# First step of the polynomial exponential on GpSimd, 32-bit shift and root times quadratic on VectorE, eight tiles a batch

## The chip, the cores and the metric

The kernel runs on one core of a Trainium2 chip. TensorE multiplies matrices into PSUM; ScalarE, VectorE and GpSimd work on tiles of 128 partitions; the DMA queues of SyncE, ScalarE and GpSimd move data. The metric is the device time of one execution in microseconds; a profile of one execution comes beside it. In the profile PE is TensorE, ACT is ScalarE, DVE is VectorE, POOL is GpSimd, SP is SyncE.

## The reference

Softcapped attention over 8 batches of 12 heads, 448 tokens, head size 64, then a soft mixture of experts with 32 slots:

```python
scores = cap * np.tanh(scale * np.matmul(q, k.T) / cap)          # cap = 30
attn = np.exp(scores - scores.max(-1)); attn /= attn.sum(-1) + 1e-09
x = np.matmul(attn, v)                    # as 3584 tokens x 768
logits = x @ phi                          # 32 slots
d = softmax of logits over the tokens; c = softmax of logits over the slots
slot_out[e] = np.maximum((d.T @ x)[e] @ w1[e], 0) @ w2[e]         # 8 experts, 4 slots each
out = c @ slot_out
```

## The kernel before

**Tiling.** A pair is two heads side by side, a quad is two pairs; there are 48 pairs. The scores of a pair come transposed, keys on partitions, in seven tiles of 128 x 448 (the line `NT = 7`). The 336 tiles are handled in 56 chunks of six, so a batch of the input (six pairs) is seven chunks, and what stands in chunk j recurs in chunk j + 7. A chunk's tiles live in one of five `ex` buffers.

**Stages of a chunk.** TensorE makes the scores of three tiles at a time (`qk_chunk`, L316) into one of two PSUM buffers `sc`. ScalarE applies tanh to the three (`tanh_chunk`, L325) and writes `ex`. One chunk later it exponentiates `ex` in place (`exp_chunk`, L329), but leaves the first `taken(j)` tiles of the chunk to VectorE. Two chunks later TensorE multiplies `ex` by V: `pv_first` does the first four tiles of a pair, `pv_rest` the others (both L385), into a single PSUM buffer of the pool `psV`. V lies in two buffers `vbd`, filled by a GpSimd cast (L286). `norm` ends a pair on VectorE: a reciprocal of the sums (L392) and a product into `xq` (L395). Then come transposes of `xq` (copied by VectorE into `xT`, L446), the logits, their exponential on ScalarE (L471), its copy on GpSimd (L477), and sums over the tokens. q and k are loaded by GpSimd's queue (L186), turned on TensorE and copied by VectorE (L278); all these turnings share one PSUM buffer, `psT`. The weights are loaded by GpSimd's queue, one or two blocks a chunk (L116, L120). After the last chunk come the two layers of the experts and the output.

**Order.** The order of the work is written by hand. The main loop runs over the chunks, and between its steps it calls slots, named `0`, `m`, `e`, `a`, `b`, `r`, `c`, `d` in this order; each slot has a part before it (`<a`) and one after it (`>a`). `at(j, slot, f, ...)` hangs a piece of work on a slot of chunk j. Each engine executes its instructions in this order and waits on semaphores; nothing is moved at run time. `FILL` hangs matrix products that compute nothing on some slots.

**The polynomial on VectorE.** From chunk 3 to chunk 53, one tile in each chunk is exponentiated with five VectorE instructions (`poly_exp`): `e` is the argument scaled to base 2 and written as a 32-bit integer (L362); the upper 16 bits shifted left by 7 are the bits of a bf16 power of two `b` (L364); the lower 16 bits are the fraction `f`, and three instructions (L365 to L367) make `((f + p2) f`, then `(. + p1) f`, then `(. + p0) b`, which is written to `ex`. There is one set of work buffers. `PARTS` says for each chunk of a batch in which slots the five stand.

**Weights.** `KEPT` blocks of w2 stay in SBUF; the others are written to DRAM as bf16 and loaded again after attention (`w2t`).

Of the kernel before, what the change touches and what calls it, by code (L numbers as in the profile page):

```python
# [9 lines left out]
F32 = mybir.dt.float32  # L10
BF16 = mybir.dt.bfloat16
I32 = mybir.dt.int32
U16 = mybir.dt.uint16
ALU = mybir.AluOpType
# [3 lines left out]
P = 128  # L18
HP = 64
NT = 7  # L20
DH = 64
S = 448
CH = 6
# [7 lines left out]

FRAC = 2.0 ** 16
POW2 = (0.07802398, 0.22606796, 0.69583329, 0.99992523)


@with_exitstack
def kernel(
# [12 lines left out]
    B, H, _, _ = q.shape  # L50
# [7 lines left out]
    cap = float(cap)  # L58
    qk_scale = 1.0 / (DH ** 0.5)

    NQB = H // 4
# [1 line left out]
    NPAIR = 2 * NQ  # L63
    NTILE = NPAIR * NT
    NCH = NTILE // CH
    KEPT = 11

    ctx.enter_context(tc.manual_schedule())
    pe, dve, act, pool, sp = nc.tensor, nc.vector, nc.scalar, nc.gpsimd, nc.sync
# [28 lines left out]
           for e in range(E - 2)]  # L98
    w2b = wts.tile([P, KEPT, 4, HD], BF16, name="w2b")

# [23 lines left out]
    w2_parts = [(n0, half) for n0 in range(0, len(blocks), 4) for half in range(2)]  # L124
    w2_kept, w2_spilled = w2_parts[:KEPT], w2_parts[KEPT:]

# [5 lines left out]

    att = ExitStack()
    ld = att.enter_context(tc.tile_pool(name="ld", bufs=1))
    NP = 1
    homes = {}
    for nm in ("qk0", "ex1", "wk", "ldv", "ex2", "ex3", "vb0", "qk1", "ex4", "ex0", "vb1"):
        homes[nm] = att.enter_context(tc.tile_pool(name=nm, bufs=1))
# [1 line left out]
    vb = [homes["vb0"], homes["vb1"]]  # L140
    qk = [homes["qk0"], homes["qk1"]]
    ldv, wk = homes["ldv"], homes["wk"]
    work = wk.tile([P, 5 * NP * S // 2], I32, name="work")
    xe, xp = work[:, 0:NP * S], work[:, NP * S:2 * NP * S].bitcast(F32)
    xb = work[:, 2 * NP * S:].bitcast(BF16)
    xs = att.enter_context(tc.tile_pool(name="xs", bufs=4))
    attp = ExitStack()
    psS = attp.enter_context(tc.tile_pool(name="psS", bufs=2, space=PSUM))
# [156 lines left out]
    scores, exs, pvs, xq, xTs, lps = {}, {}, {}, {}, {}, {}  # L305
# [25 lines left out]
    def exp_chunk(j):  # L331
        exp_part(j, taken(j), CH)

    PARTS = {0: (1, ((0, "<b", (0,)), (0, "<d", (1, 2)), (1, "a", (3,)), (1, "<b", (4,)))),
             1: (1, ((0, "<b", (0,)), (0, ">b", (1,)), (0, "c", (2,)), (1, "a", (3,)), (1, "<b", (4,)))),
             2: (1, ((0, "a", (0,)), (0, "<b", (1,)), (0, ">d", (2, 3)), (1, "a", (4,)))),
             3: (1, ((0, "a", (0,)), (0, "c", (1,)), (0, ">d", (2,)), (1, "<b", (3, 4)))),
             4: (1, ((0, ">b", (0,)), (0, "c", (1,)), (0, ">d", (2, 3)), (1, "a", (4,)))),  # L340
             5: (1, ((0, ">b", (0,)), (0, "c", (1,)), (1, "<b", (2,)), (1, ">b", (3,)), (1, "r", (4,)))),
             6: (1, ((0, ">b", (0,)), (0, "c", (1,)), (0, ">d", (2,)), (1, "a", (3,)), (1, ">b", (4,))))}
    shared = {j: (PARTS[j % 7],) for j in range(6, NCH - 6) if j % 7 in PARTS}
    shared.update({3: ((1, ((0, "a", (0,)), (0, "c", (1,)), (0, ">d", (2,)), (1, "<b", (3, 4)))),), 4: ((1, ((0, ">b", (0,)), (0, "c", (1,)), (0, ">d", (2, 3)), (1, "a", (4,)))),), 5: ((1, ((0, ">b", (0,)), (1, "a", (1, 2)), (1, "<b", (3,)), (1, ">b", (4,)))),), 50: ((1, ((0, "<b", (0,)), (0, "c", (1, 2)), (1, "a", (3, 4)))),), 51: ((1, ((0, "a", (0,)), (0, "<b", (1,)), (0, ">d", (2, 3)), (1, "a", (4,)))),), 52: ((1, ((0, ">b", (0,)), (0, "c", (1,)), (1, "a", (2,)), (1, "<b", (3, 4)))),), 53: ((1, ((0, ">b", (0,)), (0, "c", (1,)), (0, ">d", (2, 3)), (1, "a", (4,)))),)})
    if cap >= 50:
        shared = {}

    def taken(j):
        return sum(n for n, _ in shared.get(j, ()))

    lead = POW2[0] / FRAC ** 3
    p2, p1, p0 = (c / POW2[0] * FRAC ** (n + 1) for n, c in enumerate(POW2[1:]))
    halves16 = xe.bitcast(U16).rearrange("p (s two) -> p s two", two=2)
    frac, whole = halves16[:, :, 0], halves16[:, :, 1]

    def poly_exp(j, u, tiles, ops):
        n1 = tiles * S
        t = exs[j][:, u:u + tiles, :].rearrange("p u s -> p (u s)")
        e, p, b = xe[:, 0:n1], xp[:, 0:n1], xb[:, 0:n1]
        f, w = frac[:, 0:n1], whole[:, 0:n1]  # L360
        steps = (
            lambda: dve.tensor_scalar(e, t, cap * math.log2(math.e) * FRAC,  # L362
                                      (127 + math.log2(lead)) * FRAC, ALU.mult, ALU.add),
            lambda: dve.tensor_scalar(b.bitcast(U16), w, 7, None, ALU.logical_shift_left),  # L364
            lambda: dve.scalar_tensor_tensor(p, f, p2, f, ALU.add, ALU.mult),  # L365
            lambda: dve.scalar_tensor_tensor(p, p, p1, f, ALU.add, ALU.mult),  # L366
            lambda: dve.scalar_tensor_tensor(t, p, p0, b, ALU.add, ALU.mult))  # L367
        for n in ops:
            steps[n]()

# [171 lines left out]
    def at(j, slot, f, *a):  # L542
        if j < 0:
            j, slot = 0, "b"
        aux.setdefault((j, slot), []).append((f, a))
# [3 lines left out]
        busy(n, psV.tile([P, parts * P], F32, name="junk", tag="pv"))  # L549

    FILL = ((3, "a", fill, 2), (4, "a", fill, 14), (5, "a", fill, 10), (6, "a", spare, 10), (6, "c", spare, 12), (7, "a", fill, 16), (8, "a", fill, 20), (9, "a", fill, 6))
    PER = 2 * NQB * NT // CH
    assert PER == 7 and NQB == 3

    def quad_in(Q, cast_k, cast_q, k_in, q_in, v_in):
        if 0 < Q < NQ:
# [10 lines left out]
    for b in range(B):  # L567
        j, p = b * PER, 6 * b

        def when(nm):  # L570
            return j + WHEN[nm][0], WHEN[nm][1]
# [17 lines left out]
        if b < B - 1:  # L589
# [5 lines left out]
                at(*when("en"), e_norm, b)  # L595
            if b % 2:
                at(*when("es"), e_sums, b // 2)
    for j, groups in shared.items():
        u = 0
        for tiles, parts in groups:  # L600
            for dj, slot, ops in parts:
                at(j + dj, slot, poly_exp, j, u, tiles, ops)
            u += tiles
    for n, job in enumerate(wjobs):
        at(1 + n * (NCH - 5) // len(wjobs), "b", *job)
    for j, slot, n in ((0, "a", 10), (0, "c", 10), (1, "b", 10), (1, "c", 8)):
# [71 lines left out]
    assert place[last, 0] == NTILE - NT and pair_at[NCH - 3] == last - 2  # L678
    CL = CS
    exp_part(NCH - 1, taken(NCH - 1), CL)  # L680
    exp_part(NCH - 1, CL, CH - 1)
    exp_part(NCH - 1, CH - 1, CH)
# [102 lines left out]
    for n in range(12):  # L785
        a = n % 4 * NS
# [13 lines left out]
    for n0, half in sorted(w2_spilled, key=lambda x: (x[1], x[0])):  # L800
        t = tl.tile([P, 4, HD], BF16, name=f"w2t{n0}_{half}")
# [123 lines left out]
    for n in range(B // 2 * NT):  # L925
        bb, c = divmod(n, NT)
# [15 lines left out]
        if n == NH or c == 0 or full:  # L942
            ob, n1 = wts.tile([P, 2, 2, HD], F32, name="ob", tag="w1", bufs=E), n
# [44 lines left out]
```

## Time and profile before

| | |
|---|---|
| median of three runs | 302.41 us (301.85 to 303.36) |
| profiled execution: span from first to last instruction | 299.1 us |
| time of the profiled execution beside its span | not given separately; the median is 3.3 us above the span |
| TensorE, ScalarE, VectorE, GpSimd busy | 266.7, 265.7, 237.5, 139.0 us |
| exponentials on ScalarE (L329) | 58 instructions, 51 of them of five tiles |
| mean granted TensorE clock | 0.987 |

Times are microseconds from the start of the span. A busy time is the union of an engine's records; an engine's records can overlap, since the next one may start before the last has ended. A group row has the line, the engine, the operation, what it writes and reads, the shapes and the count, then busy time and mean ns of one, then the engine's idle time before them. A row of waits has the waiting engine and line, who ended the wait, the total, the count and the longest. A row of a timeline has start, duration, engine, line, operation and count. A stage row has the stretch, its length, and the busy time of PE, PEld, DVE, ACT and POOL, then the granted clock, the DMA share and GB/s.

### The profile page before, as it was taken

What the parts mean: (1) busy time and instruction counts of PE and PEld (TensorE: products, weight loads), DVE (VectorE), ACT (ScalarE), POOL (GpSimd) and SP (SyncE); (2) the same over time, 40 slices, a digit from 0 to 9 for tenths busy, and PEclk for the clock granted to TensorE, in tenths of its full rate; (3) what the DMA queues carried; (4) which work ended last, traced back from release to release, by engine and by line L of the source; (5) the groups of instructions that cost most, each with busy time, mean ns of one, the idle gap of its engine ahead of it and who ended that gap; (6) DMA issues with size and microseconds to landing.
All of it is one profiled execution on the core that took longest, in us unless ns stands there. A gap on an engine that the chain in (4) does not pass through costs nothing.

```text
span 299.1 us, 11031 instructions
## 1 busy us (share of the span) xinstructions
PE 266.7 (89%) x4821; PEld 179.3 (60%) x4821; DVE 237.5 (79%) x497; ACT 265.7 (89%) x211; POOL 139.0 (46%) x200
## 2 busy tenths in 40 slices
PE   8898989998999999989999999899999999999820
PEld 6655556755675667566756675667666767542410
DVE  3728989898999999999899989998998963336840
ACT  4999999999999999999999999999999997227730
POOL 4583554764566466745575547464653220300000
PEclk9999999999999999999999999999999999999995
DMA  7999999999999999999899999999999579929997
GB/s 230 260 192 205 200 192 205 186 198 221 229 194 181 206 231 215 197 211 227 164 179 216 228 214 183 216 228 219 192 185 223 113 246 343 400 110 354 406 422 291
DMA packets 58559, 68.12 MB, mean 228 GB/s; under 512 B 4240, under 2 KB 54672, under 8 KB 58512
## 3 DMA queue, kind: packets, MB, share of 16 engines
q0 software_dynamic: 42448, 35.31, 76.6%
q1 hardware_dynamic: 15776, 31.89, 30.3%
q8 instruction: 37, 0.61, 0.8%
q10 hardware_dynamic: 288, 0.23, 0.2%
q14 instruction: 10, 0.08, 0.1%
HBM read 91.72 MB, written 19.27 MB: 371 GB/s over the span
## 4 chain that ended last, share of the span: by engine, by line
ACT 41%; PE 32%; DVE 13%; issue 7%; POOL 2%; DMA 2%; DVEq 0%; SPq 0%; ACTq 0%
ACT ex L325 25%; ACT ex L329 13%; PE pv L385 9%; PE sc L316 5%; DVE xq L395 3%; PE so_ps L856 2%; PE hp L823 2%; PE kps L276 2%; POOL vbd L286 2%; DVE work L364 1%; PE qps L276 1%; PE xps L433 1%; PE pv L415 1%; DVE work L362 1%; ACT ob L948 1%
## 5 line engine op out<-in xcount | busy, mean ns | idle before, releaser
L325 ACT ACTIVATE ex<-sc 128x1344 bf16<-128x1344 f32 (+1 forms) x113 | 166.0, 1738 | 1.2 <-PE sc L316 1.2
L329 ACT ACTIVATE ex<-ex 128x2240 bf16<-128x2240 bf16 (+4 forms) x58 | 145.1, 2528 | 0.1
L385 PE MATMUL pv<-vbd,ex 128*128 128x130 bf16 (+1 forms) x1610 | 94.7, 211 | 8.6 <-POOL vbd L286 7.5
L385 PEld LDWEIGHTS <-ex 128*128 128x128 bf16 (+1 forms) x1680 | 76.0, 101 | 31.9 <-issue 9.2
L316 PE MATMUL sc<-qT,kT 64*64 64x448 bf16 x672 | 70.1, 359 | 2.5 <-ACT ex L325 1.9
L286 POOL CAST vbd<-vraw 64x896 bf16<-64x896 f32 x46 | 44.9, 977 | 51.1 <-PE pv L385 37.0
L366 DVE SCALAR_TENSOR_TENSOR work<-work 128x448 f32<-128x448 f32 x51 | 31.8, 623 | 1.2
L367 DVE SCALAR_TENSOR_TENSOR ex<-work 128x448 bf16<-128x448 f32 x51 | 31.8, 624 | 0.6
L365 DVE SCALAR_TENSOR_TENSOR work<-work 128x448 f32<-128x448 uint16 x51 | 31.7, 621 | 0.0
L395 DVE TENSOR_TENSOR xq<-pv,rec 128x448 bf16<-128x448 f32 x46 | 28.7, 625 | 1.6
L316 PEld LDWEIGHTS <-kT 64*64 64x64 bf16 x672 | 24.2, 105 | 7.7 <-issue 5.5
L477 POOL COPY e<-E 128x512 bf16<-128x512 bf16 x9 | 7.0, 778 | 43.0 <-PE eps L496 20.2
L364 DVE TENSOR_SCALAR work<-work 128x448 uint16<-128x448 uint16 x51 | 25.8, 506 | 0.5
L116 POOL DMA_DIRECT2D w1b<-in_moe_w_dram x32 | 24.6, 768 | 0.0
L294 POOL MEMSET vbd<- 64x1 bf16 x22 | 3.3, 149 | 42.9 <-PE pv L385 42.9
L362 DVE TENSOR_SCALAR work<-ex 128x448 int32<-128x448 bf16 x51 | 21.0, 411 | 2.1
L415 PE MATMUL pv<-ones 128*128 128x57 bf16 x502 | 20.8, 188 | 0.0
L278 DVE COPY kT<-kps 128x896 bf16<-128x896 bf16 x23 | 14.2, 619 | 7.4 <-PE kps L276 7.3
L186 POOL DMA_DIRECT2D qb<-in_q_dram x22 | 16.7, 761 | 3.1 <-DMA kraw<-in_k_dram 3.1
L415 PEld LDWEIGHTS <-ones 128*128 128x128 bf16 x502 | 17.4, 96 | 0.4
L278 DVE COPY qT<-qps 128x896 bf16<-128x896 bf16 x23 | 14.3, 624 | 3.9 <-PE qps L276 2.9
L446 DVE COPY xT<-xps 128x896 bf16<-128x896 bf16 (+1 forms) x24 | 14.4, 600 | 3.5 <-PE xps L438 3.4
(130 smaller groups left out, 332.2 us busy)
## 6 DMA issues: line engine op xcount, KB each, us to landing
w1b<-in_moe_w_dram POOLq DMA_DIRECT2D x32, 384.0 KB, 8.6
vraw<-in_v_dram SPq DMA_DIRECT2D x44, 224.0 KB, 6.1
w2d<-in_moe_w_dram POOLq DMA_DIRECT2D x21, 384.0 KB, 9.7
w2t<-w2d SPq DMA_DIRECT2D x21, 384.0 KB, 5.5
out_dram<-ob SPq DMA_DIRECT2D x7, 768.0 KB, 6.7
qb<-in_q_dram POOLq DMA_DIRECT2D x22, 224.0 KB, 7.8
kb<-in_k_dram POOLq DMA_DIRECT2D x22, 224.0 KB, 6.7
out_dram<-obh SPq DMA_DIRECT2D x23, 192.0 KB, 2.0
```

The source lines that it names most:

```text
L278: dve.tensor_copy(t, ps)
L286: pool.tensor_copy(vbds[Q % 2][r, :, :, c0:c0 + DH], raw[r])
L316: pe.matmul(sc[cs, u, 0:S], qkT["k", Q][r, c, cs], qkT["q", Q][r, :, cs], start=True, stop=True)
L325: act.activation(exs[j][:, half * CS + u0:half * CS + u1, :], sc[:, u0:u1, 0:S], ACT.Tanh, scale=qk_scale / cap)
L329: act.activation(exs[j][:, u0:u1, :], exs[j][:, u0:u1, :], ACT.Exp, scale=cap)
L364: lambda: dve.tensor_scalar(b.bitcast(U16), w, 7, None, ALU.logical_shift_left),
L365: lambda: dve.scalar_tensor_tensor(p, f, p2, f, ALU.add, ALU.mult),
L366: lambda: dve.scalar_tensor_tensor(p, p, p1, f, ALU.add, ALU.mult),
L367: lambda: dve.scalar_tensor_tensor(t, p, p0, b, ALU.add, ALU.mult))
L385: pe.matmul(out_, exs[j][r, u, q0:q0 + (HP if tail else P)], v_, start=(c == 0 and g == gs[0] < NF), stop=(c == NT - 1), skip_group_check= ...
L395: dve.tensor_tensor(xq[Q][:, h, s0:s1, :], pv[:, 0:s1 - s0, 0:DH], rec.to_broadcast([P, s1 - s0, DH]), op=ALU.mult)
L415: pe.matmul(home, ones, ones[:, 0:512 - NT * W], start=False, stop=True, skip_group_check=True)
```

## The change

The five VectorE instructions become one on GpSimd and four on VectorE.

- GpSimd (`poly_split`) scales the tile to a 32-bit integer `e`, in slot `>a` of the tile's own chunk.
- VectorE shifts `e` right by 16 and left by 23, in 32 bits, into `b`, which is then the bits of a float power of two.
- The cubic is factored into a root and a quadratic: `g = (f + root) b`, `h = (f + c1) f`, `ex = (h + c0) g`. The three instructions after the shift are of the same form as before; `g` overwrites `b`, `h` overwrites `e`.
- There are two sets of `e` and `b`, used in turn, and no separate `p`. The work buffers grow from 4,480 to 7,168 bytes a partition, and `KEPT` falls from 11 to 10.
- The slots are the same for all chunks: shift and two products in `>d` of the chunk, the last in `a` of the next (`SOLO`). `PARTS` and the lists for single chunks go.
- In the chunks 7, 14, ... 49 a second tile is taken (`DOUBLE`): shift and two products in `a` of the next chunk, the last in `<b`. So 58 tiles instead of 51 leave ScalarE, eight instead of seven in a full batch.

```diff
+ROOT = 1.838349134
+QUAD = (1.059067276, 6.971262432)
...
-    KEPT = 11
+    KEPT = 10
...
-    work = wk.tile([P, 5 * NP * S // 2], I32, name="work")
-    xe, xp = work[:, 0:NP * S], work[:, NP * S:2 * NP * S].bitcast(F32)
-    xb = work[:, 2 * NP * S:].bitcast(BF16)
+    xes = [wk.tile([P, S], I32, name=f"xe{n}") for n in range(2)]
+    xbs = [wk.tile([P, S], I32, name=f"xb{n}") for n in range(2)]
...
-    PARTS = {0: (1, ((0, "<b", (0,)), (0, "<d", (1, 2)), (1, "a", (3,)), (1, "<b", (4,)))),
...
-    shared = {j: (PARTS[j % 7],) for j in range(6, NCH - 6) if j % 7 in PARTS}
...
+    DOUBLE = (0,)
+    SOLO = ((0, ">d", (0, 1, 2)), (1, "a", (3,)))
+    NEXT = {0: ((1, "a", (0, 1, 2)), (1, "<b", (3,))),
+            3: ((1, "a", (0, 1)), (1, "<b", (2,)), (1, ">b", (3,))),
+            5: ((1, "<b", (0, 1, 2)), (1, ">b", (3,)))}
+    shared = {j: (SOLO,) + ((NEXT[j % PER],) if j % PER in DOUBLE and 5 < j < NCH - 6 else ())
+              for j in range(3, NCH - 2)}
...
+    root, c1, c0 = ROOT * FRAC, QUAD[0] * FRAC, QUAD[1] * FRAC ** 2
+    number = {x: n for n, x in enumerate((j, u) for j in sorted(shared) for u in range(taken(j)))}
+
+    def poly_buffers(j, u):
+        n = number[j, u] % 2
+        return xes[n], xes[n].bitcast(U16).rearrange("p (s two) -> p s two", two=2)[:, :, 0], xbs[n]
+
+    def poly_shift(eng, j, u):
+        e, _, b = poly_buffers(j, u)
+        eng.tensor_scalar(b, e, 16, 23, ALU.logical_shift_right, ALU.logical_shift_left)
+
+    def poly_split(j, u):
+
+        pool.tensor_scalar(poly_buffers(j, u)[0], exs[j][:, u, :], cap * math.log2(math.e) * FRAC,
+                           (127 + math.log2(lead)) * FRAC, ALU.mult, ALU.add)
+
+    def poly_exp(j, u, ops):
+        e, f, b = poly_buffers(j, u)
+        g, h, t = b.bitcast(F32), e.bitcast(F32), exs[j][:, u, :]
         steps = (
-            lambda: dve.tensor_scalar(e, t, cap * math.log2(math.e) * FRAC,
-                                      (127 + math.log2(lead)) * FRAC, ALU.mult, ALU.add),
-            lambda: dve.tensor_scalar(b.bitcast(U16), w, 7, None, ALU.logical_shift_left),
-            lambda: dve.scalar_tensor_tensor(p, f, p2, f, ALU.add, ALU.mult),
-            lambda: dve.scalar_tensor_tensor(p, p, p1, f, ALU.add, ALU.mult),
-            lambda: dve.scalar_tensor_tensor(t, p, p0, b, ALU.add, ALU.mult))
+            lambda: poly_shift(dve, j, u),
+            lambda: dve.scalar_tensor_tensor(g, f, root, g, ALU.add, ALU.mult),
+            lambda: dve.scalar_tensor_tensor(h, f, c1, f, ALU.add, ALU.mult),
+            lambda: dve.scalar_tensor_tensor(t, h, c0, g, ALU.add, ALU.mult))
...
+    for j, tiles in shared.items():
+        for u, parts in enumerate(tiles):
+            at(j, ">a", poly_split, j, u)
             for dj, slot, ops in parts:
-                at(j + dj, slot, poly_exp, j, u, tiles, ops)
-            u += tiles
+                at(j + dj, slot, poly_exp, j, u, ops)
```

## The prediction

> **What bounds the kernel now.** I read the page first, then the table of stages, the list of waits, and the timelines of single engines over one batch of seven chunks.
>
> ```profile
> PE 266.7 (89%) x4821; PEld 179.3 (60%) x4821; DVE 237.5 (79%) x497; ACT 265.7 (89%) x211; POOL 139.0 (46%) x200
> ...
> ACT  4999999999999999999999999999999997227730
> ```
>
> ScalarE is full from the second slice to the 34th, while attention runs. The table of stages, over five batches:
>
> ```profile
> 75.20:225.70 150.50, 141.91 (x2760) 99.05 (x2759) 140.57 (x295) 150.50 (x111) 87.45 (x121) 1.00 1.18 206
> ```
>
> In 150.5 us ScalarE never rests, but TensorE works 141.9 and VectorE 140.6: both have only 6% to spare, and the granted clock is full. GpSimd is at 58%. The list of waits for the same stretch says what TensorE's rest consists of:
>
> ```profile
> PE pv L385 <- POOL vbd L286: 4.6, 9, 0.9
> ...
> PE qps L276 <- DVE xT L446: 1.9, 5, 0.6
> ...
> PE sc L316 <- ACT ex L325: 1.0, 5, 0.2
> ```
>
> Only 1.0 us in five batches is a wait for ScalarE. ScalarE's timeline gives the pace:
>
> ```profile
> 99.25 2.44 ACT L329 ACTIVATE ex<-ex 128x2240 bf16<-128x2240 bf16 x1
> 101.21 2.84 ACT L325 ACTIVATE ex<-sc 128x1344 bf16<-128x1344 f32 x2
> 103.55 2.46 ACT L329 ACTIVATE ex<-ex 128x2240 bf16<-128x2240 bf16 x1
> ```
>
> The records overlap, so start to start counts: 1.96 us for an exponential of five tiles, 2.34 for two tanh, 4.30 a chunk. A batch takes 30.4 us (tanh end at 98.55, its like at 128.96). VectorE in the same stretch:
>
> ```profile
> 100.26 0.62 DVE L367 SCALAR_TENSOR_TENSOR ex<-work 128x448 bf16<-128x448 f32 x1
> 100.79 0.20 DVE L392 RECIPROCAL rec<-pv 128x7 f32<-128x7 f32 x1
> 101.02 0.62 DVE L395 TENSOR_TENSOR xq<-pv,rec 128x448 bf16<-128x448 f32 x1
> ...
> 103.72 0.39 DVE L362 TENSOR_SCALAR work<-ex 128x448 int32<-128x448 bf16 x1
> 104.14 0.39 DVE L364 TENSOR_SCALAR work<-work 128x448 uint16<-128x448 uint16 x1
> 104.67 0.20 DVE L392 RECIPROCAL rec<-pv 128x7 f32<-128x7 f32 x1
> 104.91 0.62 DVE L395 TENSOR_TENSOR xq<-pv,rec 128x448 bf16<-128x448 f32 x1
> ...
> 114.62 0.60 DVE L365 SCALAR_TENSOR_TENSOR work<-work 128x448 f32<-128x448 uint16 x1
> 115.26 0.62 DVE L366 SCALAR_TENSOR_TENSOR work<-work 128x448 f32<-128x448 f32 x1
> 115.92 0.63 DVE L367 SCALAR_TENSOR_TENSOR ex<-work 128x448 bf16<-128x448 f32 x1
> ```
>
> and TensorE:
>
> ```profile
> 101.79 0.84 PE L385 MATMUL pv<-vbd,ex 128*128 128x130 bf16 x12 [0.65 <-POOL vbd L286]
> ...
> 105.78 0.86 PE L385 MATMUL pv<-vbd,ex 128*128 128x130 bf16 x12
> ```
>
> The profile blames GpSimd's cast for the 0.65. The code says otherwise: psV has one buffer, so `pv_first` of a pair cannot start before `norm` of the pair before has read the bank. That normalisation ends at 101.02 + 0.62 = 101.64, just before 101.79; the cast then running fills the block of a later pair. So there is a loop beside ScalarE: first product, rest of product, reciprocal, normalisation, first product. From 101.79 to 105.78 TensorE goes through it without any rest, in 3.99 us, and VectorE's second normalisation ends at 105.53, 0.25 before it is needed.
>
> **What the change takes away.** Exponentials on ScalarE fall by one tile in each of seven batches (the doubled chunks are 7, 14, ... 49). The three short exponentials at the end have mean 1996, 1622 and 1247 ns for 1344, 896 and 448 elements: 0.37 us a tile. Alone that is 7 x 0.37 = 2.6 us.
>
> On VectorE each tile loses the first operation (411 ns mean) and one of the two operations before the three 0.62 products; the 16-bit shift (506 ns mean, 380 undisturbed) becomes a 32-bit one. The nearest row for that is L362, 32 bits out of 16, 380 ns undisturbed; the far bound is a product's 620, an operation at half that speed. I take 380: both undisturbed TENSOR_SCALAR groups have it. VectorE's busy time per batch goes from 7 x 2.79 = 19.5 to 8 x (0.38 + 3 x 0.62) = 17.9 us. In sum VectorE gets lighter; its order is what matters.
>
> **What it adds on GpSimd.** 58 splits of 448 elements. The cast of 896 takes 0.93 undisturbed and the copy of 512 takes 0.61, a slope that gives 0.56 for 448; a mult-add with conversion may be slower, at most the whole cast's 0.93. I take 0.6. [...] Eight splits make GpSimd 75% busy in a batch. The order of the changed kernel's instructions puts the split of a chunk behind the casts of the chunk before and ahead of the weight loads and the cast of its own chunk. It waits for the chunk's first tanh (end 102.87 for chunk 22), when the cast before has ended (101.67). The shift stands after the chunk's last copy, some 2 us later, so I cost that wait at nothing; if the cover went, every copy and normalisation behind the shift would go late with it. Loads queued behind a split move by 0.6 us: k issued at 101.62 lands about 6.7 later and is turned at 116.4, and casts are needed over 4 us after they end. Nothing for those.
>
> **What it moves: the chunk after the double.** Between the two normalisations above VectorE had 3.0 us of work, and TensorE was ready at 104.59. The new order puts there the two tiles of the doubled chunk whole: eight instructions, shift and three products twice. Each waits for the one before. Rows: 0.42 from a dependent TENSOR_SCALAR to the next (103.72 to 104.14), 0.64 and 0.66 between dependent products, 0.53 from the last to an unrelated one (100.26 to 100.79); 2.26 a tile, 4.52 for two. The product at 100.26 no longer stands ahead of the first normalisation, which so ends 0.26 earlier, at 101.39. VectorE is free at 101.31; a small reciprocal takes 0.12; 4.52 more gives 105.95 for the next reciprocal, instead of 104.67. Normalisation ends 0.86 later (104.67 to 105.53 in the row) at 106.81, TensorE starts at 106.95. That is 1.17 later than 105.78.
>
> On top, holding up. GpSimd reading SBUF stops a product:
>
> ```profile
> 237.76 0.61 POOL L477 COPY e<-E 128x512 bf16<-128x512 bf16 x1 [1.34 <-ACT E L471]
> ```
>
> ```profile
> 237.89 0.96 DVE L367 SCALAR_TENSOR_TENSOR ex<-work 128x448 bf16<-128x448 f32 x1
> ```
>
> The copy slipped in between two products, and the second took 0.96 instead of 0.62: 0.34 lost, the copy's time less 0.27. [...] In the critical window stand the split of chunk 22, which waits for the buffer that the doubled chunk's first tile frees and so starts exactly between the two tiles (0.34), and, as likely as not, the cast behind it (0.93 - 0.27 = 0.66, half of it taken). Likely delay: 1.17 + 0.34 + 0.33 = 1.84 us. Bounds: 1.17 with no hold-up, 2.17 with both.
>
> Given back in the same batch: TensorE's waits for ScalarE at 107.24 and 129.01 (0.20 + 0.12) and 0.11 of the wait for xT at 121.72, where a stretched shift (1.03 at 118.64) stood ahead of the copy. Net 1.84 - 0.43 = 1.41 a batch, bounds 0.74 and 1.74; 2.4 if the following normalisations are held up by 0.66 too. Since TensorE's loop, not ScalarE, now sets the pace, the 0.37 is lost.
>
> **What else.** KEPT falls by one: 22 instead of 21 blocks go through DRAM, 0.9 us more of loading at the end. The last block lands at 265.2 and is first read at 272.8, so nothing.
>
> **Sum.** 7 x 1.41 = 9.9 us. ScalarE has a cushion: the scores that end at 123.58 serve a tanh that ends at 125.82 and needs 1.28, so 0.96 can be lost once. Plus 8.9 on the profiled span of 299.1 gives 308.0; the median of 302.41 is 3.3 above that span, so 311.3. Bounds: 7 x 0.74 - 0.96 = 4.2, 306.6; 7 x 2.4 - 0.96 = 15.8, 318.2.
>
> **Rivals.** *Faster*: TensorE's other waits vanish and the new one is small. TensorE rests 1.6 us a batch in named waits (0.65, 0.20, 0.19, 0.32, 0.11, 0.12); if the even order of the polynomial removes all of them, the loop keeps ScalarE's pace as long as the new wait stays under 1.2 us, and 302.4 - 2.6 = 299.8. For it: VectorE's sum falls, and ScalarE has no rest at all. Against it: the window alone gives 106.95 - 105.52 = 1.43. Chance 0.12.
>
> *No change*: the eight instructions issue as unrelated ones do, 0.31 after a shift and 0.54 after a product, 3.86 in all, and nothing is held up. Then the delay is 0.51, net 0.08 a batch, inside the cushion: 302.4. Against it: they depend on each other, and dependent rows never show 0.54. Chance 0.10; a change that did not thin out ScalarE's exponentials would land here as well, but their shapes in the new order are 1792 where they were 2240.
>
> *Much slower*: VectorE becomes the bound. If every split and cast holds it up, 8 x 0.34 + 6 x 0.66 = 6.7 us a batch on 28.1 - 1.6 makes 33.2, 2.8 over 30.4: 7 x 2.8 - 0.96 = 18.6, 321.0. For it: products and shifts fill 60% of VectorE's time. Against it: in this trace only two of the 22 products that overlapped a cast or copy of GpSimd lost more than 0.3. Chance 0.08.
>
> **Numbers.** The forecast, 306 to 318, has 0.70. Slower by over 0.5% (1.5 us, about what a measurement can tell) is 0.70 + 0.08; within it 0.10; faster 0.12. The range 302 to 320 leaves out the faster case and the much slower one.
>
> **What the new profile would show.** Right: ScalarE idle in the middle of attention, waiting for scores, for the first time; a VectorE reciprocal about 1.4 to 2 us after TensorE finished its product in the chunk after each double, and TensorE's first product waiting 1.4 to 2.4 there; shifts at 0.38, splits near 0.6, some products at 0.95. Wrong: ScalarE still without rest, a batch of 30.0 us; splits over 0.9, or shifts waiting for GpSimd.

## The result, and the profile after

The changed kernel takes 330.48 us (median of four runs, 329.94 to 330.83) against 302.13 us for the kernel before on the same chip (300.65 to 303.36). The ratio is 1.096, with a 95% interval from 1.091 to 1.101. Slower was forecast, but 311.3 us and at most 320. The profiled execution has a span of 328.4 us, 29.3 more than before. Of the experiments below, the profiles of e1 and e3 are of the slowest execution of their runs (306.42 us, and 333.32 where the other three took 328.12 to 330.66), so their spans read some 1 and 3 us high, and e4's is of a disturbed execution of 363.85 us, of which nothing is read.

The page of the changed kernel, the lines that answer to those shown of before, with the row of TensorE's granted clock:

```profile
PE 276.3 (84%) x4821; PEld 186.5 (57%) x4821; DVE 257.5 (78%) x474; ACT 266.1 (81%) x211; POOL 175.9 (54%) x258
...
ACT  4999997999499959997799879996999599325840
...
PEclk9999989999699979998999989998999799999995
```

Two things are to be seen. ScalarE, which had no rest before, now has holes all through attention. And TensorE's clock, which was full before, falls in some slices. TensorE executes the same 4821 products, but is busy 276.3 us instead of 266.7, 9.6 more. It rests 328.4 - 276.3 = 52.1 us instead of 299.1 - 266.7 = 32.4, 19.7 more. The two make up the 29.3.

The chain that ended last, shares by engine (before, ScalarE 41%, TensorE 32% and VectorE 13% led it):

```profile
PE 41%; DVE 33%; issue 8%; ACT 5%; POOL 5%; DMA 4%; DVEq 0%; SPq 0%; POOLq 0%; ACTq 0%
```

TensorE's list of waits (total, times, longest) says where the rest went:

```profile
PE pv L393 <- DVE xq L403: 20.0, 12, 3.1
PE qps L276 <- DVE xT L454: 4.1, 7, 1.0
PE junk L637 <- DVE xq L403: 2.9, 1, 2.9
PE qps L276 <- DVE zacc L497: 2.4, 5, 0.8
...
PE sc L316 <- ACT ex L325: 0.5, 1, 0.5
```

The first line is the wait of `pv_first` for the normalisation. Seven waits for it are long, one behind each double: 2.16, 2.89, 2.89, 3.12, 2.12 and 2.75 us are in the first line, and the last, 2.86, is that of a fill product in the same buffer (`junk`); 18.8 in all. From the first to the last of them 207.9 us pass in six batches: 34.6 us a batch, where it was 30.4.

VectorE's timeline in the chunk behind one double (start, duration):

```profile
110.09 0.62 DVE L403 TENSOR_TENSOR xq<-pv,rec 128x448 bf16<-128x448 f32 x1
110.63 0.20 DVE L515 RECIPROCAL winv<-wps 128x7 f32<-128x7 f32 x1
110.75 0.95 DVE L361 TENSOR_SCALAR xb<-xe 128x448 int32<-128x448 int32 x1
111.73 0.62 DVE L373 SCALAR_TENSOR_TENSOR xb<-xe,xb 128x448 f32<-128x448 uint16 x1
112.39 0.63 DVE L374 SCALAR_TENSOR_TENSOR xe<-xe 128x448 f32<-128x448 uint16 x1
113.12 0.63 DVE L375 SCALAR_TENSOR_TENSOR ex<-xe,xb 128x448 bf16<-128x448 f32 x1
113.66 0.39 DVE L361 TENSOR_SCALAR xb<-xe 128x448 int32<-128x448 int32 x1
114.08 0.87 DVE L373 SCALAR_TENSOR_TENSOR xb<-xe,xb 128x448 f32<-128x448 uint16 x1
114.99 0.62 DVE L374 SCALAR_TENSOR_TENSOR xe<-xe 128x448 f32<-128x448 uint16 x1
115.65 1.32 DVE L375 SCALAR_TENSOR_TENSOR ex<-xe,xb 128x448 bf16<-128x448 f32 x1
116.90 0.19 DVE L400 RECIPROCAL rec<-pv 128x7 f32<-128x7 f32 x1
117.12 0.62 DVE L403 TENSOR_TENSOR xq<-pv,rec 128x448 bf16<-128x448 f32 x1
```

GpSimd's timeline there, of which three lines matter:

```profile
110.50 0.94 POOL L286 CAST vbd<-vraw 64x896 bf16<-64x896 f32 x1
...
113.92 0.55 POOL L365 TENSOR_SCALAR xe<-ex 128x448 int32<-128x448 bf16 x1 [1.81 <-DVE ex L375]
...
115.55 0.95 POOL L286 CAST vbd<-vraw 64x896 bf16<-64x896 f32 x1
```

And TensorE's timeline, the first products of the two pairs (the later one waited):

```profile
110.86 0.85 PE L393 MATMUL pv<-vbd,ex 128*128 128x130 bf16 x12 [0.44 <-DVE winv L515]
...
117.81 0.86 PE L393 MATMUL pv<-vbd,ex 128*128 128x130 bf16 x12 [2.89 <-DVE xq L403]
```

The eight instructions stand between the two normalisations as forecast. Three of them are stretched, each where an instruction of GpSimd lies beside it: the shift to 0.95 (its like is 0.39), a product to 0.87 and a product to 1.32 (their likes are 0.62). The loop from first product to first product takes 117.81 - 110.86 = 6.95 us, where it took 3.99. The seven loops of this kind are 6.21, 6.94, 6.95, 7.17, 6.17, 6.80 and 6.90 us (the last up to the fill product), 6.73 in mean.

The table of stages for the five microseconds behind that wait; the third figure from the right is the granted clock:

```profile
118.00:119.00 1.00, 1.00 (x30) 0.95 (x29) 0.96 (x3) 0.00 (x0) 0.69 (x1) 0.97 1.16 191
119.00:120.00 1.00, 1.00 (x17) 0.30 (x9) 0.97 (x2) 0.16 (x1) 0.00 (x0) 0.50 0.93 115
120.00:121.00 1.00, 1.00 (x18) 0.83 (x15) 0.90 (x3) 1.00 (x1) 0.00 (x0) 0.50 1.04 228
121.00:122.00 1.00, 1.00 (x18) 0.80 (x17) 0.47 (x1) 0.14 (x1) 0.00 (x0) 0.50 1.19 222
122.00:123.00 1.00, 1.00 (x24) 0.47 (x17) 0.81 (x2) 0.29 (x1) 0.84 (x1) 0.82 1.25 208
```

A microsecond after TensorE has resumed, its clock falls to 0.50 for 3.4 us. TensorE is busy all that time, but with 17 or 18 products in each whole microsecond where the one ahead has 30, and ScalarE, which needs its scores, stands still for most of it. The same follows each of the seven doubles (it starts between 0.4 us before and 1.2 us after TensorE resumes, and lasts 6.8 us once); in the kernel before, no microsecond between 10 and 290 has a clock under 0.97, and the longest pause of TensorE there is 0.92 us. That step was in no part of the prediction.

### The profile page after: what moved, and what is told of

Its sections match the earlier page's. It is cut to its first block, busy times and chain, and to the rows that moved or that the text cites. A ratio compares the mean times of both kernels' runs of the same rounds, so it can differ in the third digit from the quotient of the medians.

```text
span 328.4 us, 11140 instructions
## 1 busy us (share of the span) xinstructions
PE 276.3 (84%) x4821; PEld 186.5 (57%) x4821; DVE 257.5 (78%) x474; ACT 266.1 (81%) x211; POOL 175.9 (54%) x258
## 4 chain that ended last, share of the span: by engine, by line
PE 41%; DVE 33%; issue 8%; ACT 5%; POOL 5%; DMA 4%; DVEq 0%; SPq 0%; POOLq 0%; ACTq 0%
PE pv L393 15%; DVE xe L374 7%; DVE xb L373 7%; PE sc L316 6%; DVE xb L361 5%; DVE ex L375 4%; DVE xq L403 4%; PE qps L276 3%; POOL vbd L286 2%; ACT ex L325 2%; DMA vraw<-in_v_dram 2%; PE kps L276 2%; PE so_ps L861 2%; PE hp L828 2%; ACT ex L329 1%
## 5 line engine op out<-in xcount | busy, mean ns | idle before, releaser
L325 ACT ACTIVATE ex<-sc 128x1344 bf16<-128x1344 f32 (+1 forms) x113 | 141.3, 1294 | 24.3 <-PE sc L316 24.0
L329 ACT ACTIVATE ex<-ex 128x2240 bf16<-128x2240 bf16 (+5 forms) x58 | 116.5, 2014 | 0.1
L286 POOL CAST vbd<-vraw 64x896 bf16<-64x896 f32 x46 | 44.1, 959 | 29.3 <-PE pv L393 24.0
L365 POOL TENSOR_SCALAR xe<-ex 128x448 int32<-128x448 bf16 x58 | 37.6, 649 | 35.1 <-DVE ex L375 20.0
L374 DVE SCALAR_TENSOR_TENSOR xe<-xe 128x448 f32<-128x448 uint16 x58 | 41.3, 712 | 2.0
L375 DVE SCALAR_TENSOR_TENSOR ex<-xe,xb 128x448 bf16<-128x448 f32 x58 | 39.9, 688 | 3.6
L373 DVE SCALAR_TENSOR_TENSOR xb<-xe,xb 128x448 f32<-128x448 uint16 x58 | 39.7, 685 | 2.0
L361 DVE TENSOR_SCALAR xb<-xe 128x448 int32<-128x448 int32 x58 | 31.6, 545 | 0.0
L276 PEld LDWEIGHTS <-qb 128*64 128x64 bf16 x308 | 11.0, 111 | 14.9 <-issue 14.9
L400 DVE RECIPROCAL rec<-pv 128x7 f32<-128x7 f32 x46 | 9.4, 204 | 12.8 <-PE pv L393 12.4
L276 PE MATMUL qps<-ident,qb 128*64 128x128 bf16 x308 | 13.1, 224 | 7.0 <-DVE xT L454 4.1
```

What stands on the lines that cost most here:

```text
L276: pe.transpose(ps[h * HP:h * HP + HP, c, :], src[:, h, c * DH:(c + 1) * DH], ident)
L286: pool.tensor_copy(vbds[Q % 2][r, :, :, c0:c0 + DH], raw[r])
L325: act.activation(exs[j][:, half * CS + u0:half * CS + u1, :], sc[:, u0:u1, 0:S], ACT.Tanh, scale=qk_scale / cap)
L329: act.activation(exs[j][:, u0:u1, :], exs[j][:, u0:u1, :], ACT.Exp, scale=cap)
L361: eng.tensor_scalar(b, e, 16, 23, ALU.logical_shift_right, ALU.logical_shift_left)
L373: lambda: dve.scalar_tensor_tensor(g, f, root, g, ALU.add, ALU.mult),
```

## The experiments

Three theories and a rival were tried. **Theory 1**: the instructions that stand ahead of a normalisation make TensorE wait. **Theory 2**: the pause drops the clock, and that costs on top. **Theory 3**: GpSimd's hold-ups make a large part of the window. **Rival R**: the moves to GpSimd themselves cost, wherever the eighth tile stands.

| Run | Median us | Ratio to before, 95% interval | Span of the profile | TensorE busy | Rest | Mean clock |
|---|---|---|---|---|---|---|
| before | 302.13 | 1 | 299.1 | 266.7 | 32.4 | 0.987 |
| after | 330.48 | 1.091 to 1.101 | 328.4 | 276.3 | 52.1 | 0.946 |
| e1_single | 304.95 | 1.005 to 1.016 | 303.6 | 265.1 | 38.5 | 0.988 |
| e2_fill | 324.20 | 1.069 to 1.079 | 322.1 | 282.5 | 39.6 | 0.985 |
| e3_moved | 330.40 | 1.085 to 1.099 | 331.3 | 281.5 | 49.8 | 0.925 |
| e4_old_double | 328.61 | 1.080 to 1.093 | - | - | - | - |
| e5_spread | 327.70 | 1.080 to 1.096 | 324.2 | 266.1 | 58.1 | 0.979 |
| e6_slots | 302.05 | 1.000 to 1.005 | 299.5 | 265.2 | 34.3 | 0.982 |
| e7_nocast | 318.97 | 1.053 to 1.063 | 315.8 | 269.9 | 45.9 | 0.966 |
| e8_old_double_again | 329.56 | 1.085 to 1.101 | 326.9 | 283.9 | 43.0 | 0.911 |
| e9_free | 300.78 | 0.998 to 1.003 | 298.1 | 264.3 | 33.8 | 0.984 |
| e10_thin | 326.20 | 1.074 to 1.086 | 323.7 | 273.6 | 50.1 | 0.946 |

Rest is span less TensorE's busy time. Ratios go by runs of the kernel before on the same chip; beside the experiments these had medians from 300.8 to 301.6.

**e1_single: no eighth tile.**

```
-    DOUBLE = (0,)
+    DOUBLE = ()
```

> The changed kernel without its eighth tile: GpSimd's split, the 32-bit shift, the root times a quadratic and the uniform slots stay, but no chunk has a second VectorE tile (51 tiles, as before; ScalarE does 7 more exponentials than in the changed kernel). Theory 1 (the eight polynomial instructions of the chunk after the double stand ahead of the normalisation, and TensorE's first product waits for it): with four instructions there, one of them hidden, the normalisation is as early as before, no wait of over 1 us of TensorE for xq stays, the granted clock is about 0.99 as before, and the time is that of the kernel before, 300 to 304 us. Rival R (the moves to GpSimd themselves cost: 51 splits that hold VectorE up, in-order waits, the uniform slots): 315 us or more, with VectorE or TensorE waits all over the batch.

Measured: 304.95 us. No long wait for xq is left and the clock is full. Rival R falls: 51 splits on GpSimd, the new shift and the new order cost some 3 us together (304.95 against 301.57 for the kernel before), and 25 of the 28 us come with the eighth tile. 304.95 is 0.95 above the upper end that theory 1 gave; e6 says whose the 3 us are.

**e2_fill: TensorE kept busy while it waits.**

```
+    def warm(n):
+        busy(n, psT.tile([P, 3 * P], F32, name="warm", tag="T"))
...
-    FILL = (..., (9, "a", fill, 6))
+    FILL = (..., (9, "a", fill, 6), (8, "d", warm, 45))
```

> The changed kernel with 15 products of 384 columns more (2.5 us, on constants, into a bank that is free there; they compute nothing that is used) on TensorE in the chunk after the double, just ahead of the place where it waits 2.1 to 3.1 us for the normalisation. The wait for xq is as late as before, but TensorE is busy through most of it. Theory 2 (the pause drops TensorE's granted clock to 0.50 for some 4 us, and the batch's next scores and products come 1.6 us late for that): the granted clock stays at 0.9 or more behind the wait, the scores of the next chunk come 1.3 to 1.6 us earlier per batch, and the time is 318 to 321 us. Rival (the slow stretch is hidden behind ScalarE or VectorE, only the wait itself counts): 328 to 331 us.

Measured: 324.20 us, 6.3 less, with 105 products more, 15 in each of seven batches. TensorE's timeline in that place:

```profile
111.12 2.61 PE L637 MATMUL warm<-ones 128*128 128x384 bf16 x15
...
114.91 0.84 PE L393 MATMUL pv<-vbd,ex 128*128 128x130 bf16 x12 [0.23 <-DVE xq L403]
...
118.64 0.58 PE L276 MATMUL qps<-ident,qb 128*64 128x128 bf16 x14 [0.38 <-DVE kT L278]
```

The loop is as long as it was (107.98 to 114.91, 6.93 us), no microsecond between 10 and 290 has a clock under 0.97, and the stretch from the waiting product to the q transposes takes 118.64 - 114.91 = 3.73 us instead of 122.59 - 117.81 = 4.78. So the clock loss is real, 6.3 us of the time, and the rival falls. The gain is smaller than forecast, since TensorE, now on time, meets VectorE's next two late results: 0.38 for kT, and 0.28 for xq behind it. The changed kernel shows neither, so the slow clock had hidden them. A batch takes 33.9 us (81.05 to 114.91).

**e3_moved: the eighth tile where no normalisation follows.**

```
-    DOUBLE = (0,)
+    DOUBLE = (5,)
```

> The changed kernel with the second tile of each batch in another chunk: the one behind which no normalisation stands (two polynomials lie there between normalisations that are two chunks apart, a stretch of some 7 us by the order of the instructions). As many instructions on every engine as in the changed kernel. Theory 1: the normalisations are in time, the 2.1 to 3.1 us waits for xq go, with them the clock loss, and the time is 302 us, at most 312. Rival R (an eighth tile costs the same wherever it stands, because VectorE has no room for it or GpSimd holds it up): 326 to 332 us.

Measured: 330.40 us, the time that this run's rival gave: an eighth tile costs the same in this place too. Theory 1 as I had put it is wrong: the waits for xq went, as it says, but the time stayed. TensorE's timeline shows the wait that took their place:

```profile
107.80 0.33 PE L493 MATMUL zps<-ones,e 128*128 128x1 bf16 x4 [2.44 <-DVE kT L278]
```

The copy of k from PSUM now stands behind the two polynomials on VectorE, and psT has one buffer, just as psV has. So TensorE waits 2.4 us for kT in place of 2.9 for xq, and the clock falls behind it as before (0.50 from 108 to 114). The amended theory: VectorE has a duty for TensorE, whether normalisation or copy, at least every 3.9 us (101.02 to 104.91 is one of the longest stretches between two in the kernel before), and an extra tile ahead of any of them is a pause of TensorE. e5 and e10 try it in two more places.

**e4_old_double and e8_old_double_again: the kernel before, with an eighth tile all on VectorE.**

```
-             1: (1, ((0, "<b", (0,)), (0, ">b", (1,)), (0, "c", (2,)), (1, "a", (3,)), (1, "<b", (4,)))),
+             1: (1, ((0, "c", (0, 1, 2)), (1, "a", (3,)), (1, "<b", (4,)))),
...
-    shared = {j: (PARTS[j % 7],) for j in range(6, NCH - 6) if j % 7 in PARTS}
+    TWO = (1, ((1, "a", (0, 1, 2, 3, 4)),))
+    shared = {j: (PARTS[j % 7],) + ((TWO,) if j % 7 == 0 else ()) for j in range(6, NCH - 6) if j % 7 in PARTS}
```

(The last operations of the first tile in the doubled chunk were moved ahead by a place as well.)

> The kernel before, with all five polynomial instructions on VectorE and nothing on GpSimd, and only a second VectorE tile added in the same chunk of each batch as in the changed kernel (five instructions more ahead of the normalisation there). Theory 1 says that it is the queue of instructions ahead of that normalisation, whichever engine does the split: TensorE waits about 2 us per batch for xq, the granted clock drops behind it, and the time is 313 to 322 us. Rival R (the loss is the split's, by its hold-ups on VectorE): at most 306 us.

> The kernel before with a second VectorE tile in the same chunk, once more, since the profile of its first run was a disturbed one (clock 0.65, 362 us, against 327 to 329 us in the timed runs). Theory 1 with theory 2: 327 to 330 us, waits of over 2 us of TensorE for xq once per batch and a granted clock of 0.5 behind them, though GpSimd does no part of a polynomial here. Rival: the loss is spread over the batch and no wait for xq is longer than 1 us.

Measured: 326.92, 328.03 and 329.19 us in three executions of e4 (and 363.85 in the one that was profiled), and 329.56 in e8, the median of two. e8's lines, the page's clock, TensorE's waits, and the product that waited:

```profile
PEclk9999987999699959996999789977998699999985
```

```profile
PE pv L386 <- DVE xq L396: 12.6, 7, 2.0
```

```profile
115.61 1.48 PE L386 MATMUL pv<-vbd,ex 128*128 128x130 bf16 x12 [2.00 <-DVE xq L396]
```

With no polynomial work on GpSimd the eighth tile costs as much. The wait is the 2.0 us that theory 1 gave. The clock, though, falls for 6.8 us behind each of the seven pauses, twice as long as behind most in the changed kernel, and TensorE is busy 283.9 us, 17.2 more than before. e4's 313 to 322 had the clock in at the price seen in the changed kernel; TensorE is busy 7.6 us more here than there, about what the upper end lacked.

**e5_spread: the eighth tile cut in two by a normalisation.**

```
-    NEXT = {0: ((1, "a", (0, 1, 2)), (1, "<b", (3,))),
+    NEXT = {0: ((1, "a", (0, 1)), (1, "c", (2, 3))),
...
```

> The changed kernel with the second tile of the double cut in two: its shift and root product stay ahead of the normalisation of the next chunk, its quadratic and last product go behind that normalisation, so ahead of the one after it. The same instructions, some 1.1 us ahead of each of two normalisations instead of 2.3 us ahead of one. In the run with one tile a chunk, a normalisation ends only 0.15 to 0.25 us before TensorE's next product at most places, so theory 1 says that nearly all of it comes back: two waits of some 1 us each for xq (or for a transposed copy behind it). Theory 2 says that pauses this short leave the granted clock at 0.97 or more. Both together: 318 to 323 us. If the clock falls behind two short pauses as it does behind the long one: 328 us or more. If half the tile fits into gaps of VectorE: 308 to 314 us.

Measured: 327.70 us, 5 above the forecast. Two pauses became three, TensorE's timeline of one batch:

```profile
114.63 0.86 PE L393 MATMUL pv<-vbd,ex 128*128 128x130 bf16 x12 [0.86 <-DVE xq L403]
117.07 0.58 PE L276 MATMUL kps<-ident,kb 128*64 128x128 bf16 x14 [0.79 <-DVE xT L454]
120.66 0.58 PE L276 MATMUL qps<-ident,qb 128*64 128x128 bf16 x14 [1.80 <-DVE kT L278]
```

That is 3.45 us, more than the one pause of 2.89. The clock kept full behind all of them but one, a wait of 2.67 us for kT in the first of the seven batches (TensorE is busy 266.1 us, 1.0 more than in e1). So pauses this short (up to 2.05 us) left the clock alone here, as theory 2 has it; e7 shows shorter ones (1.51 us) that did not. TensorE is busy 10.2 us less than in the changed kernel, but rests 6.0 more: 58.1 us, the most of any run and 19.6 more than in e1, 2.8 a batch. That is above the 2.26 us that the prediction's rows give for a tile's four instructions, so VectorE had no gap to take them in.

**e6_slots: one tile a chunk, in the places of before.** The lists of places of the kernel before are put back, without the operation that GpSimd does:

```
+    shared = {j: tuple(tuple((dj, slot, tuple(n - 1 for n in ops if n)) for dj, slot, ops in p)
+                       for _, p in g) for j, g in shared.items()}
```

> One tile a chunk, first operation on GpSimd, 32-bit shift and root times quadratic, but each remaining VectorE instruction in the place that its counterpart had in the kernel before (the run with one tile a chunk and uniform places was 1.1% slower than the kernel before). Theory: those 3.4 us are the uniform places', which let zacc's addition and a copy of k end 0.4 to 0.8 us later than before where TensorE waits for them; then this is 300 to 302.5 us, bound by ScalarE as before. Rival (the 3.4 us are GpSimd's hold-ups of VectorE, some 0.24 us a split, and shifts that wait for the split): 304 to 307 us.

Measured: 302.05 us, ratio 1.0021 (0.9996 to 1.0047). So the three microseconds of e1 were the uniform places', and TensorE's lists agree: in e1 it waits 2.6 us for zacc and 2.5 for kT, in e6 not at all for zacc and 0.3 for kT. GpSimd's split, the 32-bit shift and the root times a quadratic cost nothing that can be measured when each instruction keeps its place; nor does keeping ten parts of w2 instead of eleven. They gain nothing either, though VectorE's busy time falls from 237.5 to 232.4 us.

**e7_nocast: GpSimd's two casts taken out of the window.**

```
-        pool.tensor_copy(vbds[Q % 2][r, :, :, c0:c0 + DH], raw[r])
+        d = 1 if Q and Q % NQB == 0 else DH
+        pool.tensor_copy(vbds[Q % 2][r, :, :, c0:c0 + d], raw[r][:, :, :, 0:d])
```

> The changed kernel with GpSimd's casts of v cut to one column for the first head group of each batch (that v is not filled in), which are the two casts that stood beside the shift and the last product of the window behind the double (0.95 instead of 0.38 us, 1.32 instead of 0.63). Theory 3 (hold-ups by GpSimd make about 1.2 us of the window): the normalisation there comes 1.1 to 1.3 us earlier, TensorE's wait falls from about 2.7 to about 1.5 us per batch, the clock drop shrinks with it, and the time is 315 to 321 us. Rival (the window is set by the count of instructions; the hold-ups only move): 327 us or more.

Measured: 318.97 us, 11.5 less, as theory 3 said. VectorE's timeline, and then TensorE's: shift and last product are back at their own length, only the product beside the split is long.

```profile
106.02 0.34 DVE L362 TENSOR_SCALAR xb<-xe 128x448 int32<-128x448 int32 x1
...
108.75 0.87 DVE L374 SCALAR_TENSOR_TENSOR xb<-xe,xb 128x448 f32<-128x448 uint16 x1
109.66 0.62 DVE L375 SCALAR_TENSOR_TENSOR xe<-xe 128x448 f32<-128x448 uint16 x1
110.31 0.62 DVE L376 SCALAR_TENSOR_TENSOR ex<-xe,xb 128x448 bf16<-128x448 f32 x1
110.86 0.20 DVE L401 RECIPROCAL rec<-pv 128x7 f32<-128x7 f32 x1
```

```profile
106.14 0.84 PE L394 MATMUL pv<-vbd,ex 128*128 128x130 bf16 x12 [0.44 <-DVE winv L516]
...
111.77 0.86 PE L394 MATMUL pv<-vbd,ex 128*128 128x130 bf16 x12 [1.58 <-DVE xq L404]
```

The loop is 111.77 - 106.14 = 5.63 us, 1.32 less than with the casts; the pause is 1.58 instead of 2.89. The clock falls behind three of seven pauses. So the 11.5 us are not the hold-ups' alone: TensorE is also busy 6.4 us less than in the changed kernel.

**e9_free: what the eighth tile could bring at most.**

```
     def taken(j):
-        return len(shared.get(j, ()))
+        return len(shared.get(j, ())) + (j % PER == 0 and 5 < j < NCH - 6)
```

> The kernel with the old places (one VectorE tile a chunk, split on GpSimd), in which ScalarE also skips the second tile of each doubled chunk, and no engine computes that exponential (left out: 7 tiles keep the tanh). It asks what the eighth tile could bring at most, if VectorE did it in no time. If ScalarE alone bounds that kernel: 7 x 0.37 = 2.6 us less than the run with the old places, 299.0 to 300.0 us. If the loop of first product, normalisation and first product, with its 0.05 to 0.25 us to spare, sets the pace as much as ScalarE does: 301.0 to 302.5 us, no gain that can be measured, and the eighth tile had nothing to win.

Measured: 300.78 us over twelve runs, and 1.0003 (0.9975 to 1.0032) of the kernel before. It lies between the two expectations. Against e6 it is 1.27 us less by the medians, but the two ran on different chips; by their ratios to the kernel before, 1.0003 and 1.0021, it is 0.5 us less, and the intervals overlap. So some 0.5 to 1.3 of the 2.6 us come, which isn't clear of noise. The chain that ended last has 41% on ScalarE in the kernel before, 29% in e6 and 8% in e9. ScalarE's groups from 75.2 to 225.7 us show the same, by form (busy, mean ns), first of the kernel before, then of e6, then of e9:

```profile
L325 ACT ACTIVATE ex<-sc 128x1344 bf16<-128x1344 f32 x70 | 107.7, 1878 | 0.0
```

```profile
L325 ACT ACTIVATE ex<-sc 128x1344 bf16<-128x1344 f32 x70 | 93.8, 1470 | 0.0
```

```profile
L325 ACT ACTIVATE ex<-sc 128x1344 bf16<-128x1344 f32 x71 | 90.8, 1337 | 0.2
```

The tanh of 1344 elements has records of 1878, 1470 and 1337 ns, though the pace hardly changes. A record can start while the one before it still runs (in the kernel before an exponential ends at 101.69 us, and the tanh behind it starts at 101.21), so I read the longer records as instructions that were ready early; no run tests this reading by itself. By it ScalarE's work comes later in e6 than before, and just in time in e9. ScalarE fills its row in all three (150.50, 150.48 and 150.29 of 150.5 us busy), so its row at nine tenths can't tell them apart; the mean of one form can.

**e10_thin: the old places, with the eighth tile laid between the duties one or two instructions at a time.**

```
+    TWO = ((1, "a", (0,)), (1, "<b", (1,)), (1, "c", (2,)), (2, "a", (3,)))
+    shared = {j: g + ((TWO,) if j % PER == 0 and 5 < j < NCH - 6 else ()) for j, g in shared.items()}
```

> The old places once more, with the eighth tile as it would be laid most gently there: its shift and root product in different places ahead of the next normalisation, its quadratic and last product in different places behind it. VectorE has about 2.3 us more in a stretch where each of its duties for TensorE ends only 0.05 to 0.25 us before it is needed. Theory 1: most of that comes back as several waits of 0.3 to 1.2 us, 12 to 20 us in all, with no fall of the clock: 313 to 322 us. If VectorE's 0.9 us gaps take it in: 303 to 307 us. If the clock falls as well: over 325 us.

Measured: 326.20 us. TensorE's timeline of one batch:

```profile
117.29 0.86 PE L399 MATMUL pv<-vbd,ex 128*128 128x130 bf16 x12 [1.25 <-DVE xq L409]
122.99 0.58 PE L276 MATMUL qps<-ident,qb 128*64 128x128 bf16 x14 [2.32 <-DVE kT L278]
```

The delay adds up behind the second half of the tile, where the copy of kT is due, and the clock falls in five of the seven batches (TensorE is busy 8.4 us more than in e6), so the third of the expectations came. Each place tried for a whole eighth tile cost 22 us or more over the run without it, and even free of cost it would bring about 1. None of the runs beats the kernel before by more than can be measured.

## Why the prediction was right or wrong, point by point

The prediction had the sign, the place and the mechanism: the chunk behind the double, the single buffer of psV, eight instructions ahead of the normalisation, ScalarE idle and waiting for scores for the first time. It forecast 8.9 us more than before, and 28.4 came.

Three runs, each with one thing more, take this apart by their medians. e1 (the uniform places alone) is 3.4 us above its kernel before; e2 (the eighth tile with it, the clock kept full) is 19.3 above e1, if the fill itself costs nothing; the changed kernel is 6.3 above e2. The sum is 29.0, since the kernel before took 0.6 less beside e1 and e2 than beside the changed kernel. For the three the forecast had -4.8 (7 times the 0.43 given back and the 0.26 by which the first normalisation was to end earlier), 14.7 (7 times 2.10, the longer loop) and nothing, and it took off 1.0 for the cushion. So it was short by 8.2 for the places, 4.6 for the loop, 6.3 for the clock and 1.0.

- **The instructions of the window** (0.42, 0.64, 0.66, 0.53, so 4.52 for two tiles) were right. In e7, without casts, they take 110.86 - 106.02 = 4.84 us, of which 0.25 is the split's hold-up: 4.59.
- **The hold-ups were mis-sized.** The sum had 0.34 for the split and half of 0.66 for one cast, 0.67. The timeline shows 0.25 for the split, 0.56 for the cast beside the shift, which had no term at all, and 0.70 for the cast beside the last product: 1.51. The forecast's window alone made the loop 1.43 us longer (the figure stands among its rivals; 1.17 is what is left when the first product starts 0.26 earlier), so 2.10 with the hold-ups. This loop came 2.96 longer, 0.86 more, and 0.84 of that are these hold-ups; e7 gave 1.32 back when both casts went. Over all seven loops the mean is 2.74 longer, since the last product met its cast in five of them; something of GpSimd stretched the shift in all seven (0.75 to 1.07 us). That was to be seen: in the program a cast stands behind the last products of each of the two pairs (`vcast_after`), and the prediction itself names a shift of 1.03 us (at 118.64). The size of one hold-up, from an operation of GpSimd 0.55 or 0.94 long, fits what the prediction read off before: the stretched last product ends 0.47 us after the cast beside it (116.97 and 116.50), as the product of before ended 0.48 after the copy (238.85 and 238.37), and the stretched shift 0.26 after its cast (111.70 and 111.44).
- **The clock was not foreseen**, and that is the step that failed outright: it had no term. "The granted clock is full" was read off the stages of a kernel without long pauses and kept for one with a pause of 2 to 3 us in every batch. TensorE is busy 9.6 us more than before for the same products, and 11.2 more than in e1. e2 shows it from the other side: with the pause filled and the loop as long, TensorE's busy time less 105 products of 0.163 us (start to start; 17.1) is 265.4, as in e1 (265.1). It gave back 6.3 us and not 11.2, since some of the slow stretch had hidden other waits.
- **The credits did not come.** 0.43 a batch, 3.0 in all, were to be given back by waits that vanish. The waits for ScalarE did (0.5 us in all are left), but one for zacc came (2.4), and those for xT rose from 2.4 to 4.1. The wait that the profile puts down to winv is no new one: `wps` lies in psT, the product waits for psV, and it starts 0.15 after the first normalisation's end at 110.71; it is 0.44 where the kernel before had 0.65. The places of the remaining tiles are what is behind this: e1 and e6 differ in nothing else, and by 2.9 us. The prediction costed the places in one window and left the other six chunks of each batch at nothing.
- **ScalarE's cushion** of 0.96 us was taken off the sum; with TensorE late in every batch no run shows it by itself.
- **Small terms were right.** A split alone takes 0.55 to 0.56 us (0.6 was taken), a shift 0.38. No shift waits for a split in the changed kernel: idle time ahead of the shifts is 0.0 in their group. It is the splits that wait: GpSimd idles 35.1 us ahead of them, 20.0 of it for VectorE. The twenty-second part of w2 cost nothing that can be measured, since e6 has it too.
- **The rival "faster"** (0.12) lost more than its chance tells: e9 has some 0.5 to 1.3 us to win, not 2.6. The rival "much slower" gave 321.0 from VectorE as the bound; over the span VectorE is no nearer to full (78% where it was 79%), and it is its stretches between two duties that are.
- **The range** reached to 320.0. The forecast with the clock's 6.3 us added is 317.6, still inside; with the loop's 4.6 as well it is 322.2. So the clock alone does not explain the miss: e2, with a full clock, took 324.20 us.

## What to carry to other kernels

A busy share of 94% isn't 6% of room: ask for each duty of the helping engine how long before its use it ends (in the kernel before, five of a batch's six normalisations end 0.14 to 0.25 us before the product that needs them), and count an extra instruction ahead of it as a pause of the waiting engine, whichever duty it stands ahead of. When a change puts a pause into TensorE's stream (here those of 1.5 to 3.1 us were mostly followed by 3.4 or 6.8 us at a granted clock of 0.50), price what comes behind the pause as well, and test the price with products that compute nothing, put where it waits. Before work is moved off a full engine, leave that work out altogether in one run: here this would have shown about 1 us to win, where each place tried lost 22 or more.

## What the runs showed of the hardware

TensorE's granted clock fell to 0.50 behind many pauses of 1.3 to 3.1 us in these runs, and each time for 3.4 or 6.8 us. In e7 the slow stretches start at 79.02, 143.88 and 212.14 us. These are worked out from the clock in stages of one microsecond, such as

```profile
79.00:80.00 1.00, 1.00 (x23) 0.67 (x20) 0.95 (x2) 1.00 (x1) 0.91 (x2) 0.51 1.25 206
...
82.00:83.00 1.00, 1.00 (x17) 0.47 (x15) 0.29 (x2) 0.00 (x0) 0.21 (x1) 0.78 1.24 219
```

where 0.51 is 0.02 us at 1.00 and 0.98 at 0.50, the values of the whole stages around, and 0.78 is 0.44 at 0.50 and 0.56 at 1.00. The stretch lasts from 79.02 to 82.44, 3.42 us. The second and the third start come 64.86 and 133.12 us after the first, 19.0 and 39.0 times 3.41. In the changed kernel the starts are 47.27, 81.40, 118.95, 153.08, 187.22, 221.35 and 255.48 us, 11 times 3.41 apart once (37.55) and 10 times otherwise (34.13 or 34.14). Every slow stretch of after, e3, e5, e7, e8 and e10 that starts before 290 us lasts 3.4 or 6.8 us, once or twice that step. Slow stretches sum up to 27.2 us in the changed kernel, 47.7 in e8 and 13.7 in e7, and TensorE's busy time is 11.2, 18.8 and 4.8 us over that of e1, 0.35 to 0.41 us for each slow microsecond.

The clock fell at pauses of 1.3 us (e3, one that no engine is named for), 1.51 us (e7), 2.00 us (e8) and 2.1 to 3.1 us (after). It did not fall behind four other pauses of e7, of 1.5 to 1.6 us, or six of e5, of 1.8 to 2.05 us. What decides below some 2 us stays open; of the pauses over 2.1 us in these runs, all but one (2.32 us in e10) brought the clock down.

The hold-ups between VectorE and GpSimd also reach an instruction with a single tile as input: the 32-bit shift took 0.95 us beside a cast, where it takes 0.38 alone.
